# Down projection with weights stationary, two token groups at a time, and seven block products for eight in half of the feature blocks

## The chip, the cores and the metric

The kernel runs on one core of a Trainium2 chip. The metric is the device time of one execution, in microseconds (us); the median of three runs stands for a kernel. The engines are TensorE (PE, with its weight loads PEld), VectorE (DVE), ScalarE (ACT), GpSimd (POOL) and SyncE (SP), which issues nearly all DMA transfers here.

## The reference

A linear attention with decay in blocks of 64 positions gives the tokens, and an MLP with a leaky ReLU follows:

```python
batch, n_heads, seq, head_dim = (4, 8, 768, 64)
for b in range(nb):                       # blocks of 64 positions
    ...
    out[:, :, sl] = intra + inter
    kv_state = lam_block[None, :, None, None] * kv_state + np.einsum('bhsd,bhse->bhde', kb_dec, vb)
# bridge: (B,H,S,D) -> (B*S, H*D)
n_tokens, d_model, d_ff = (3072, 512, 2048)
h = x @ w_in
g = np.maximum(0.01 * h, h)
return (g @ w_out).astype(np.float32)
```

All values are float32. The change concerns the last product, `g @ w_out`: 3,072 tokens by 2,048 features by 512 columns.

## The kernel before

**Three parts for each operand.** The products run on TensorE in a 4-byte float type with fewer significant bits (fp32r). Each operand is therefore written as three such tiles, called h, l and m: h is the operand scaled (by `NEAR`, just below 1) and rounded, l is what h lost, and m is a combination of h and l. Each product of two operands is three matmuls, h by h, l by l and m by m, and the scales are chosen so that a weighted sum of the three is the product to float32 accuracy. `parts` makes them for the weights (ACT or DVE for h, L591 or L593; DVE for l, L596, and m, L602), and `down_load` for the features (ACT L682, DVE L683 and L685).

**Stages.** The attention rounds (chunks of 128 positions) fill the tokens x group by group: six groups of 512 tokens (`NG`, `T`). The features are cut into eight blocks p of 256 (`NP`). `up(g, p)` (L640) multiplies one group by one block of `w_in`, with the weights stationary and 512 tokens streaming; ACT rescales between the m products and the others (L658) and applies the leaky ReLU (L661), and the result `gs` goes to memory as `G[g][p]`, 512 KB with features on the partitions, two halves of 128. Rounds and up blocks are interleaved. Meanwhile `w_out` arrives as words of eight bytes, becomes float32 (`to_float32`, ACT and DVE, from the buffer `raw0`), goes to memory as `WO[p]`, and is read back and split by `w_out_parts` in the last token group of the up stage, after which the weight tiles `W[p]` hold parts of `w_out` instead of `w_in`.

**The down stage** starts when the up stage ends. For each group g and each pair of feature blocks, `down_load` fetches `G[g][p]` into a buffer `graw`, lying where the attention had its tiles, and splits it into one of four ring slots (`NR`), which lie in the two buffers X that the up stage read tokens from (slots 0 and 1 in X[0], 2 and 3 in X[1]). `down` (L700) then multiplies: the stationary operand is a slot's 128 features by 128 tokens, and 512 columns of `W[p]` stream. Each block of 128 tokens has two of the eight PSUM banks, one for h and l and one for m; a bank is complete after all eight feature blocks. Then ACT rescales the first bank into a buffer in SBUF (L722), DVE adds the second to it (L729), and SP stores 256 KB, 128 tokens by 512 columns (L732). The very last block is done in two halves of 256 columns.

**Order.** The class `Plan` takes every instruction with an assumed duration, the names that it reads and writes, and a rank (its place in the list `seq`), and plans by these assumed times which instruction each engine takes next; the instructions are then emitted in the planned order. Each engine works in that order, so an instruction that has to wait holds up all that is behind it on its engine. SP's queue is of this kind too. Loads of the down stage have the rank of eight steps earlier (`plan.rank = n - 8.0`). `move` adds a DMA with a slack that delays its planned place.

Of the kernel before, what the change touches and what calls it, by code (L numbers as in the profile page):

```python
# [8 lines left out]
F32 = mybir.dt.float32  # L9
# [16 lines left out]
S = 4096.0  # L26
# [136 lines left out]
def kernel(  # L163
# [34 lines left out]

    DV = 10
# [21 lines left out]
    bank = {"b10": b1[0], "b11": b1[1], "b2": b2}  # L221
# [3 lines left out]
    raw = [sb([P, 2 * d_model], f"raw{i}") for i in range(NRAW)]  # L225
    lows = [sb([P, d_model], f"low{i}", I32) for i in range(2)]
    w32 = sb([P, 2, d_model], "w32")
    w32f = w32.rearrange("p h n -> p (h n)")
    tt = [raw[-1][:, i * T:(i + 1) * T] for i in range(2)]
    gs = [sb([P, 2, T], f"gs{i}") for i in range(2)]  # L230
    WO = [dram.tile([P, 2 * d_model], F32, name=f"wo{p}", tag=f"wo{p}") for p in range(NP)]
    G = [[dram.tile([P, 2 * T], F32, name=f"g{g}_{p}", tag=f"g{g}_{p}") for p in range(NP)] for g in range(NG)]
# [323 lines left out]
    def to_float32(kind, p, h, dst, key, after=()):  # L556
# [20 lines left out]
        move(1.6, get, after, [f"raw{j}"])  # L577
# [9 lines left out]
    def parts(p, src, keys):  # L587
        wh, wl, wm = W[p]
        def head(e):
            if e == "ACT":  # L590
                nc.scalar.activation(out=wh, in_=src, func=AF.Copy, bias=0.0, scale=NEAR / S)  # L591
            else:
                nc.vector.tensor_scalar(wh, src, NEAR / S, None, op0=ALU.mult)  # L593

        add(("ACT", "DVE"), (1.05, 0.7), head, keys, [f"wh{p}"])
        add("DVE", 1.25, lambda: nc.vector.scalar_tensor_tensor(wl, wh.bitcast(F32), -S, src, op0=ALU.mult, op1=ALU.add),  # L596
            keys + [f"wh{p}"], [f"wl{p}"])
        difference(p)
# [12 lines left out]
    NR = 4  # L611
    graw = [att[:, j * 2 * T:(j + 1) * 2 * T] for j in range(NR)]

# [5 lines left out]
    def w_out_parts(p):  # L619
        j = p % NR  # L620
        add("DMA", 1.5, lambda: nc.sync.dma_start(out=graw[j], in_=WO[p]), [f"WO{p}"], [f"gr{j}"], rank=-3.0)
        parts(p, graw[j], [f"gr{j}"])


    n_t = n_g = 0
    n_b = -EARLY

    def up(g, p, lo=0, hi=GC):
# [20 lines left out]
        for fs in blocks:  # L649
# [11 lines left out]
            add("ACT", ns, lambda b=b, r=r: nc.scalar.activation(out=r, in_=b, func=AF.Prelu, bias=0.0, scale=1.0 / WS, alpha=0.01),  # L661
# [6 lines left out]
    acc = [[z[:, i].rearrange("p y t -> p (y t)") for i in range(2)] for z in (psc, po)] + [  # L668
        [b1[0], b2], [b1[1], pt.rearrange("p y t -> p (y t)")]]
    ACC = [["psc", "psc"], ["po", "po"], ["b10", "b2"], ["b11", "pt"]]  # L670
    ring = [[X[j // 2][z].rearrange("p k t -> p (k t)")[:, j % 2 * 2 * T:(j % 2 + 1) * 2 * T] for z in range(3)] for j in range(NR)]

    def down_load(g, p):
        j = (g * NP + p) % NR
        add("DMA", 1.5, lambda: nc.sync.dma_start(out=graw[j], in_=G[g][p]), [f"G{g}{p}"], [f"gr{j}"])
        h, l, m = ring[j]
        reads = [f"gr{j}"]

        def wr(z):
            return [f"r{z}{j}"] + [f"x{z}{j // 2}{cc}" for cc in range(GC)] if g == 0 and p < NR else [f"r{z}{j}"]  # L680

        add("ACT", 1.05, lambda: nc.scalar.activation(out=h, in_=graw[j], func=AF.Copy, bias=0.0, scale=NEAR), reads, wr("h"))  # L682
        add("DVE", 1.25, lambda: nc.vector.scalar_tensor_tensor(l, graw[j], 1.0, h.bitcast(F32), op0=ALU.mult, op1=ALU.subtract),  # L683
            reads + [f"rh{j}"], wr("l"))
        add("DVE", 1.25, lambda: nc.vector.scalar_tensor_tensor(m, l.bitcast(F32), -S, h.bitcast(F32), op0=ALU.mult, op1=ALU.add),  # L685
            [f"rh{j}", f"rl{j}"], wr("m"))

    def down(g, p):

        nonlocal n_t  # L690
        for tb in range(GC):
            done = p + 2 == NP
            very_last = done and g == NG - 1 and tb == GC - 1

            def go(pps, zs, cols, tb=tb):
                for pp in pps:
                    j = (g * NP + pp) % NR
                    for f in range(2):
                        for z in zs:
                            nc.tensor.matmul(acc[tb][z // 2][:, cols], lhsT=ring[j][z][:, f * T + tb * P:f * T + (tb + 1) * P],  # L700
                                             rhs=W[pp][z][:, f * d_model:(f + 1) * d_model][:, cols],
                                             start=pp == 0 and f == 0 and z != 1, stop=pp == NP - 1 and f == 1,
                                             skip_group_check=True)

            def needs(pps, zs):
                return [f"{x}{z}{y}" for pp in pps for z in zs for x, y in (("r", (g * NP + pp) % NR), ("w", pp))]


            every = slice(0, d_model)
            halves = [slice(0, d_model // 2), slice(d_model // 2, d_model)]  # L710
            one, two = (p,), (p + 1,)
            order = [(one, (0, 1, 2), every), (two, (0, 1, 2), every)]
            if very_last:
                order = [(one + two, (0, 1), every)] + [(one + two, (2,), x) for x in halves]
            for pps, zs, cols in order:
                part_of = f"{halves.index(cols)}" if cols in halves else ""
                add("PE", 0.227 * 2 * len(pps) * len(zs) * (0.53 if part_of else 1.0), lambda pps=pps, zs=zs, cols=cols, go=go: go(pps, zs, cols),
                    needs(pps, ["hlm"[z] for z in zs]) + ([ACC[tb][1]] if part_of else []), sorted({ACC[tb][z // 2] + part_of for z in zs}))
            if done:
                jt, n_t = n_t % 2, n_t + 1  # L720
                t, y = tt[jt], gs[jt][:, 0, :]
                add("ACT", 0.6, lambda t=t, tb=tb: nc.scalar.activation(out=t, in_=acc[tb][0], func=AF.Copy, bias=0.0, scale=(1.0 + 1.0 / S) / U),  # L722
                    [ACC[tb][0]], [f"t{jt}"], rank=-1.5)
                rows = out[(g * GC + tb) * P:(g * GC + tb + 1) * P, :]
                n = 2 if very_last else 1
                for i in range(n):
                    cols = slice(i * d_model // n, (i + 1) * d_model // n)
                    add("DVE", 0.69 / n + 0.08 * (n - 1),
                        lambda t=t, y=y, tb=tb, cols=cols: nc.vector.scalar_tensor_tensor(  # L729
                            y[:, cols], acc[tb][1][:, cols], 1.0 / WS, t[:, cols], op0=ALU.mult, op1=ALU.add),  # L730
                        [f"t{jt}", ACC[tb][1]] + ([ACC[tb][1] + str(i)] if n == 2 else []), [f"gs{jt}{i}" if n == 2 else f"gs{jt}"], rank=-1.5)
                    add("DMA", 0.8 / n, lambda rows=rows, y=y, cols=cols: nc.sync.dma_start(out=rows[:, cols], in_=y[:, cols]),  # L732
                        [f"gs{jt}{i}" if n == 2 else f"gs{jt}"], [], rank=-1.5)

# [83 lines left out]
```

## Time and profile before

| | |
|---|---|
| runs | 610.41, 611.12, 612.04 us; median 611.12 |
| span of the profiled execution | 609.2 us from the first to the last instruction (the median time lies 1.9 us above it) |
| mean granted clock of TensorE | 0.999 |
| busy in the span | PE 98%, PEld 81%, DVE 52%, ACT 44%, POOL 14% |
| the chain that ended last | PE 92%, DVE 4%, DMA 2%, ACT 1% |
| down stage | 343.4 to 605.6 us, PE busy throughout |
| moved | 105.18 MB, mean 173 GB/s |

A share of busy time is an average over stages. In the tables by stretch, each row gives start:end in us, the length, then busy us and number of instructions of PE, PEld, DVE, ACT and POOL, the granted clock, the share of time that the 16 DMA engines were busy, and GB/s. In the groups, a row gives line, engine, operation, out<-in, shape and count, then busy us and the mean ns of one, then the idle time just before them and what ended most of it. A row of the timeline gives the start, the length, the engine and the line, with the idle time before it in brackets. A row of the DMA issues gives the count, the size of each and the median us from issue to landing.

### The profile page before, as it was taken

What the parts mean: (1) busy time and instruction counts of PE and PEld (TensorE: products, weight loads), DVE (VectorE), ACT (ScalarE), POOL (GpSimd) and SP (SyncE); (2) the same over time, 40 slices, a digit from 0 to 9 for tenths busy, and PEclk for the clock granted to TensorE, in tenths of its full rate; (3) what the DMA queues carried; (4) which work ended last, traced back from release to release, by engine and by line L of the source; (5) the groups of instructions that cost most, each with busy time, mean ns of one, the idle gap of its engine ahead of it and who ended that gap; (6) DMA issues with size and microseconds to landing.
All of it is one profiled execution on the core that took longest, in us unless ns stands there. A gap on an engine that the chain in (4) does not pass through costs nothing.

```text
span 609.2 us, 12932 instructions
## 1 busy us (share of the span) xinstructions
PE 597.9 (98%) x5386; PEld 495.6 (81%) x5386; DVE 314.0 (52%) x418; ACT 269.0 (44%) x430; POOL 86.8 (14%) x90
## 2 busy tenths in 40 slices
PE   7899999999999999999999999999999999999997
PEld 6687888888888878888788888888888888888886
DVE  5999764334243426326366745545454544635531
ACT  4688974444455646555577522222222313214111
POOL 1654412104133004104000000000000000000000
PEclk9999999999999999999999999999999999999999
DMA  9998774667888878886686843524333343333201
GB/s 213 232 272 245 221 203 124 173 133 199 199 213 238 212 227 214 216 244 210 233 300 217 290 145 103 173 69 139 138 104 131 112 138 105 138 104 122 86 1 69
DMA packets 147754, 105.18 MB, mean 173 GB/s; under 512 B 123632, under 2 KB 124400, under 8 KB 147696
## 3 DMA queue, kind: packets, MB, share of 16 engines
q1 hardware_dynamic: 147552, 104.36, 58.9%
q8 instruction: 42, 0.69, 0.5%
q14 instruction: 16, 0.13, 0.1%
q10 hardware_dynamic: 144, 0.00, 0.0%
HBM read 68.69 MB, written 35.65 MB: 171 GB/s over the span
## 4 chain that ended last, share of the span: by engine, by line
PE 92%; DVE 4%; DMA 2%; ACT 1%; issue 0%; POOL 0%; SPq 0%; DVEq 0%; ACTq 0%
PE b L640 40%; PE b L700 18%; PE po L700 11%; PE psc L700 11%; PE po L313 4%; PE pt L700 4%; PE psc L313 4%; DMA g<-gs 1%; DMA att<-in_v_dram 1%; DVE w L584 1%; DVE w L585 1%; DVE wm L602 1%; PE pt L403 1%; DMA att<-in_k_dram 1%; DVE wl L596 0%; DVE wh L593 0%
## 5 line engine op out<-in xcount | busy, mean ns | idle before, releaser
L682 ACT ACTIVATE xh<-att 128x1024 fp32r<-128x1024 f32 x48 | 50.7, 1060 | 148.7 <-PE b L700 140.7
L683 DVE SCALAR_TENSOR_TENSOR xl<-att,xh 128x1024 fp32r<-128x1024 f32 x48 | 58.6, 1223 | 98.6 <-ACT xh L682 98.6
L640 PE MATMUL b<-xm,wm 128*128 128x512 f32 (+2 forms) x392 | 104.5, 393 | 0.5 <-ACT b L658 0.5
L640 PE MATMUL b<-xl,wl 128*128 128x512 f32 (+2 forms) x392 | 103.4, 388 | 0.6 <-DVE wl L596 0.6
L640 PE MATMUL b<-xh,wh 128*128 128x512 f32 (+2 forms) x392 | 103.2, 387 | 0.8 <-ACT xh L507 0.8
L640 PEld LDWEIGHTS b<-xh,wh 128*128 128x128 f32 x392 | 73.0, 188 | 15.9 <-ACT xh L507 0.9
L640 PEld LDWEIGHTS b<-xl,wl 128*128 128x128 f32 x392 | 72.8, 188 | 15.6 <-DVE wl L596 1.0
L640 PEld LDWEIGHTS b<-xm,wm 128*128 128x128 f32 x392 | 71.5, 188 | 15.7 <-ACT b L658 0.9
L658 ACT ACTIVATE b<-b 128x512 f32<-128x512 f32 (+2 forms) x97 | 56.1, 580 | 60.3 <-PE b L640 60.1
L661 ACT ACTIVATE gs<-b 128x512 f32<-128x512 f32 (+2 forms) x97 | 56.8, 591 | 44.9 <-PE b L640 38.8
L700 PE MATMUL b<-wl,xl 128*128 128x512 f32 x192 | 74.8, 390 | 0.0
L700 PE MATMUL b<-wh,xh 128*128 128x512 f32 x192 | 74.8, 390 | 0.0
L685 DVE SCALAR_TENSOR_TENSOR xm<-xl,xh 128x1024 fp32r<-128x1024 f32 x48 | 58.7, 1226 | 4.7
L462 POOL TENSOR_TENSOR att<-att 128x256 f32<-128x256 f32 x40 | 35.0, 876 | 57.2 <-DVE att L459 55.9
L700 PEld LDWEIGHTS b<-wl,xl 128*128 128x128 f32 x192 | 36.1, 188 | 7.4
L700 PEld LDWEIGHTS b<-wh,xh 128*128 128x128 f32 x192 | 36.0, 188 | 7.5
L423 POOL TENSOR_TENSOR att<-att 128x512 f32<-128x512 f32 (+1 forms) x20 | 24.2, 1211 | 96.2 <-DVE att L383 47.4
L452 DVE TENSOR_TENSOR att<-psc,att 128x512 f32<-128x512 f32 x24 | 16.5, 690 | 41.0 <-PE psc L313 41.0
L584 DVE TENSOR_SCALAR w<-w 128x512 int32<-128x512 int32 x32 | 19.2, 599 | 35.4 <-ACT w L578 35.3
L700 PE MATMUL po<-wm,xm 128*128 128x512 f32 x96 | 37.4, 390 | 0.0
L700 PE MATMUL po<-wh,xh 128*128 128x512 f32 x96 | 37.4, 390 | 0.0
L700 PE MATMUL po<-wl,xl 128*128 128x512 f32 x96 | 37.4, 390 | 0.0
(73 smaller groups left out, 805.4 us busy)
## 6 DMA issues: line engine op xcount, KB each, us to landing
att<-g SPq DMA_DIRECT2D x48, 512.0 KB, 3.3
g<-gs SPq DMA_DIRECT2D x47, 512.0 KB, 4.0
raw<-in_moe_w_in_dram SPq DMA_DIRECT2D x16, 512.0 KB, 5.4
raw<-in_moe_w_out_dram SPq DMA_DIRECT2D x16, 512.0 KB, 4.7
att<-in_k_dram SPq DMA_DIRECT2D x48, 128.0 KB, 4.2
att<-in_v_dram SPq DMA_DIRECT2D x24, 256.0 KB, 4.4
out_dram<-gs SPq DMA_DIRECT2D x23, 256.0 KB, 2.1
wo<-w SPq DMA_DIRECT2D x8, 512.0 KB, 5.9
```

The lines of the kernel that those rows point to most:

```text
L313: nc.tensor.matmul(dst[HALF[cols]], lhsT=lhsT[HALF[rows]], rhs=rhs[HALF[rows]], start=start, stop=True, skip_group_check=True)
L423: add(eng, us, lambda: e.tensor_tensor(o, x, _bc(pow_q, 2, 2)[:, :, m, :], op=ALU.mult), ["fq", dep], [f"qsT{i}"])
L452: add("DVE", 0.69, lambda: nc.vector.tensor_tensor(sc, psc[:, :, lower, :], decay, op=ALU.mult), ["psc", "fk"], ["sc"])
L462: add("POOL", 0.7, lambda new=new, j=j: nc.gpsimd.tensor_tensor(state[(j + 1) % 4], new, _bc(lam_c, 2, D), op=ALU.mult), [f"st{j % 4}", "f ...
L584: add("DVE", 0.42, lambda: nc.vector.tensor_scalar(d, d, 3, None, op0=ALU.logical_shift_left), [], [key])
L640: nc.tensor.matmul(dst, lhsT=w[z][:, kk * 2 * P + f * P:kk * 2 * P + (f + 1) * P], rhs=x[z][:, kk, toks], start=start and kk == 0, stop=kk ...
L658: add("ACT", ns, lambda b=b: nc.scalar.activation(out=b, in_=b, func=AF.Copy, bias=0.0, scale=S + 1.0), [], [kb], rank=-1.5)
L661: add("ACT", ns, lambda b=b, r=r: nc.scalar.activation(out=r, in_=b, func=AF.Prelu, bias=0.0, scale=1.0 / WS, alpha=0.01), [kb], [f"gs{jg} ...
L682: add("ACT", 1.05, lambda: nc.scalar.activation(out=h, in_=graw[j], func=AF.Copy, bias=0.0, scale=NEAR), reads, wr("h"))
L683: add("DVE", 1.25, lambda: nc.vector.scalar_tensor_tensor(l, graw[j], 1.0, h.bitcast(F32), op0=ALU.mult, op1=ALU.subtract), reads + [f"rh{ ...
L685: add("DVE", 1.25, lambda: nc.vector.scalar_tensor_tensor(m, l.bitcast(F32), -S, h.bitcast(F32), op0=ALU.mult, op1=ALU.add), [f"rh{j}", f" ...
L700: nc.tensor.matmul(acc[tb][z // 2][:, cols], lhsT=ring[j][z][:, f * T + tb * P:f * T + (tb + 1) * P], rhs=W[pp][z][:, f * d_model:(f + 1) ...
```

## The change

The down stage is written anew.

- **Weights stationary, banks transposed.** A bank now holds 128 output columns by the 512 tokens of a group. The stationary operand is a quarter of `W[p]`, and a ring slot streams (`product`). All three matmuls of a product go to one bank, since the m part is made with the factor of its product folded in (`minus`, in place of the one instruction of `difference`: a subtraction on DVE or POOL and a scaling on ACT); the leaky ReLU's scale takes up the rest. So a group of tokens needs four banks, and a pair of groups all eight, called X, Z, Y, V, two of each kind.
- **Seven for eight.** Two groups by two halves of the columns by two halves of the features make a 2x2 block product. For p < 4 (`NS`) it is done with seven block products (`strassen`, units t = 1 to 7 with u = 0, 1 for the two pairs of p; 12 matmuls of 512 columns each) in place of eight. Their operands are sums and differences: of the weights, made in `w_out_parts` (four subtractions of 256 columns per p, L661, and three extra parts in the freed attention and `low` buffers), and of G, made in `sums_of`: two loads of 512 KB, four subtractions of 512 columns on DVE or POOL, two stores of 512 KB to `TS`. There are twelve sets of these, one for each pair of groups and p < 4: the four of pair 0 late in the up stage, those of pairs 1 and 2 during the down stage. Between the units banks are copied (`copy_banks`, ACT) or added (`add_banks`, ACT and then DVE). For p >= 4 `plain` does the ordinary 24 matmuls for each group.
- **Loads.** `unit` loads straight into the m tile of a ring slot (two transfers of 256 KB for a unit of `strassen`, one of 512 KB for `plain`) and splits there: one ACT and two DVE instructions as before. The ring has four slots in pair 0, and a fifth after it, in the freed `raw` buffers. In pair 0 the first units use the slots 0, 1, 0, 1, 2, 3.
- **Leaving.** `leave` transposes a bank by blocks of 32 x 32 on DVE into one of the two halves of `gs0` and stores it by four DMAs of 32 partitions, in pieces of 32 columns (128 bytes). There are 24 banks to store; the very last is done in two halves.
- The first step of `w_out`'s conversion comes one place earlier, and its loads have the slack 0.75 in place of 4.0.

The core of the diff:

```diff
-    tt = [raw[-1][:, i * T:(i + 1) * T] for i in range(2)]
+    TS = [[dram.tile([P, 4 * T], F32, ...) for p in range(NS)] for r in range(NG // 2)]
...
+    def minus(us, x, key):
+        add(("DVE", "POOL"), (us, 1.9 * us), lambda e: ENG[e].tensor_tensor(x(2), x(1).bitcast(F32), x(0).bitcast(F32), op=ALU.subtract), ...)
+        add("ACT", 0.85 * us, lambda: nc.scalar.activation(out=x(2), in_=x(2).bitcast(F32), func=AF.Copy, bias=0.0, scale=1.0 / (S + 1.0)), ...)
...
-    acc = [[z[:, i].rearrange("p y t -> p (y t)") for i in range(2)] for z in (psc, po)] + [...]
+    acc = {"X": flat[:2], "Z": flat[2:], "Y": [b1[0], b2], "V": [b1[1], bank["pt"]]}
+    KINDS = {1: (0, "X"), 5: (1, "V"), 6: (-1, "Z"), 2: (2, "X"), 7: (-2, "Z"), 3: (-3, "Y"), 4: (3, "Z")}
+    BANKS = [[("X", 0), ("X", 1), ("Z", 0), ("Z", 1)], [("Y", 0), ("Y", 1), ("V", 0), ("V", 1)]]
+    slots = [0, 1] + [0, 1, 2, 3] * 4
...
+    def unit(pieces):
+        def go():
+            a = 0
+            for _, src, lo, n in pieces:
+                nc.sync.dma_start(out=ring[j][2][:, a:a + n].bitcast(F32), in_=src[:, lo:lo + n])
+                a += n
...
+        add("DMA", 1.5, go, [x[0] for x in pieces], wr("m"))
+        add("ACT", 1.05, head, [f"rm{j}"], wr("h"))
+        add("DVE", 1.25, low, [f"rm{j}", f"rh{j}"], wr("l"))
+        add("DVE", 1.25, middle, [f"rh{j}", f"rl{j}"], [f"rm{j}"])
...
+    def sums_of(pr, p):
+        for z, kz, g in ((a, ka, 2 * pr), (b, kb, 2 * pr + 1)):
+            move(1.5, lambda z=z, g=g: nc.sync.dma_start(out=z, in_=G[g][p]), [f"G{g}{p}"], kz, slack=WSLACK)
+        for o, u, v, w in ((a[0], b[0], a[0], ka), (b[0], b[1], b[0], kb), (b[1], b[1], a[0], kb), (a[1], a[1], b[1], ka)):
+            add(SUM[0], SUM[1], lambda e="POOL", o=o, u=u, v=v: ENG[e].tensor_tensor(o, u, v, op=ALU.subtract), [], ka + kb)
+        for z, kz, i in ((x[0], ka, 0), (y[0], kb, 1)):
+            move(1.5, lambda z=z, i=i: nc.sync.dma_start(out=TS[pr][p][:, i * 2 * T:(i + 1) * 2 * T], in_=z), kz, ...)
+    def product(dst, j, col, lhs, first=False, n=T):
+        for z in range(3):
+            nc.tensor.matmul(dst, lhsT=lhs(z), rhs=ring[j][z][:, col:col + n], start=first and z == 0, stop=z == 2, ...)
...
+    def leave(g, c, b, kb, k, lo, n):
+        o, n_o = n_o % 2, n_o + 1
+        y = gs[0][:, o, lo:lo + n]
+        add("DVE", 0.1 + 0.6 * n / T, lambda: nc.vector.transpose(out=y, in_=b[:, lo:lo + n]), [kb, k], ...)
+        def store():
+            for a in range(4):
+                nc.sync.dma_start(out=out[g * T + lo:g * T + lo + n, c * P + a * C4:c * P + (a + 1) * C4].rearrange("(b i) j -> i b j", i=C4),
+                                  in_=y[a * C4:(a + 1) * C4, :].rearrange("i (b j) -> i b j", j=C4))
+    def add_banks(d, s):
+        for i in range(2):
+            add("ACT", 0.6, lambda i=i, y=y: nc.scalar.copy(y, acc[s][i]), [ACC[s][i]], key, rank=-1.5)
+            add("DVE", 0.72, lambda i=i, y=y: nc.vector.tensor_tensor(acc[d][i], acc[d][i], y, op=ALU.add), [f"o{i}"], [ACC[d][i]], rank=-1.5)
...
+        if pr:
+            seq += [late[0], s(1, 0), late[1], s(1, 1), ("copy", "Z", "X"), late[2], s(6, 0), late[3], s(6, 1), ("copy", "Y", "Z"),
+                    s(5, 0), s(5, 1), ("add", "Y", "V"), s(7, 0), s(7, 1), ("add", "V", "Z"),
+                    s(3, 0), *soon[0], n(4, 0), s(2, 0), n(5, 0), *soon[1], s(3, 1), s(2, 1), n(6, 0), *soon[2], s(4, 0), s(4, 1), *soon[3], n(7, 0)]
+        else:
+            i = seq.index(("up", NG - 1, NP - 1))
+            seq[i:i] = [s(1, 0)]
+            seq += [s(1, 1), ("copy", "Z", "X"), s(2, 0), s(2, 1), s(3, 0), s(3, 1), s(6, 0), s(6, 1), ("add", "Y", "Z"),
+                    s(5, 0), s(5, 1), ("add", "Y", "V"), ("wp", 4), s(7, 0), s(7, 1), ("add", "V", "Z"), ("wp", 5),
+                    *soon[0], n(4, 0), s(4, 0), *soon[1], ("wp", 6), n(5, 0), s(4, 1), *soon[2], ("wp", 7), n(6, 0), *soon[3], n(7, 0)]
+    seq += [n(p, 1) for p in range(NS, NP)]
```

Lines of the changed kernel that are named below: loads of a ring slot L741, its splits on ACT L746 and on DVE L750 (l) and L754 (m); subtractions of `minus` L610 and its scaling L612; `sums_of` L772 (loads), L775 (subtractions) and L777 (stores); bank copies L857 and additions L862 (ACT) and L863 (DVE); the transposes of `leave` L846 and its stores L850.

Counted in the built order, the down stage had 1,148 matmuls of 512 columns and 8 of 256 (L700); it now has 1,074 and 12 (L781) and two that open banks (L807). The splits of ring steps go from 48 to 66, the loads of ring steps from 48 to 108 DMAs, the stores of the output from 25 to 100, and 24 loads and 24 stores of `sums_of` are new.

## Prediction before the run

> **What bounds the kernel now.** I read the page's head first, then the stretch of the down stage by engine, then its groups and its end. The page's busy row and clock row:
>
> ```profile
> span 609.2 us, 12932 instructions
> PE 597.9 (98%) x5386; PEld 495.6 (81%) x5386; DVE 314.0 (52%) x418; ACT 269.0 (44%) x430; POOL 86.8 (14%) x90
> PEclk9999999999999999999999999999999999999999
> ```
>
> TensorE works 98% of the span at full clock, so only fewer matmuls can save time, and any wait added costs its full length. The table by stretch (the last column pair is DMA share and GB/s; the third row is the down stage):
>
> ```profile
> 130.00:132.00 2.00, 2.00 (x10) 1.68 (x9) 0.96 (x3) 0.73 (x2) 0.00 (x0) 1.00 0.45 71
> 440.00:470.00 30.00, 30.00 (x134) 24.87 (x133) 15.04 (x13) 7.36 (x8) 0.00 (x0) 1.00 0.33 106
> 343.40:605.60 262.20, 262.20 (x1161) 217.26 (x1159) 128.58 (x118) 63.50 (x72) 0.00 (x0) 1.00 0.34 116
> ```
>
> The down stage has no PE wait at all: 262.2 us for 1,148 matmuls of 512 columns and 8 of 256. DVE is half used, POOL idle, DMA at a third. 48 matmuls take 10.88 us in the chain of waits, **0.2267 us each**. The groups that the change multiplies, and the waits of the loads' first step:
>
> ```profile
> L682 ACT ACTIVATE xh<-att 128x1024 fp32r<-128x1024 f32 x48 | 50.7, 1060 | 148.7 <-PE b L700 140.7
> L683 DVE SCALAR_TENSOR_TENSOR xl<-att,xh 128x1024 fp32r<-128x1024 f32 x48 | 58.6, 1223 | 98.6 <-ACT xh L682 98.6
> L685 DVE SCALAR_TENSOR_TENSOR xm<-xl,xh 128x1024 fp32r<-128x1024 f32 x48 | 58.7, 1226 | 4.7
> L452 DVE TENSOR_TENSOR att<-psc,att 128x512 f32<-128x512 f32 x24 | 16.5, 690 | 41.0 <-PE psc L313 41.0
> L383 DVE STREAM_TRANSPOSE att<-att 128x512 f32<-128x512 f32 x11 | 7.2, 678 | 1.1 <-DMA att<-in_q_dram 1.1
> ```
>
> ACT waited 140.7 us for PE to free a ring slot: loads and splits are far ahead. One ring step of 512 KB costs ACT 1.06 and DVE 2.45 us.
>
> **What is removed.** In the built order the 1,148 full matmuls become 1,076 (two of them only open banks), the 8 half ones 12. A half one is 0.139 us (8 in 1.11 us, below). 72 x 0.2267 = 16.3, less 4 x 0.139 = 0.6: **-15.8 us**, 262.2 to 246.4. L722 and L729 (25 outputs) also go, both hidden.
>
> **What is added, and where it is hidden.** Ring steps go from 48 to 66: 18 x 2.45 = 44.1 us of DVE. With 20 of the 48 sum subtractions (0.69 by L452), 14 bank additions (0.69) and the weight sums, DVE in the down stage rises from 128.6 to about 207 of 246 us, an estimate from these rows. That average is below one, but the order is uneven. I counted the built order in steps of 96 matmuls (21.8 us of PE), at row prices. DVE gets 20.0 and 20.3 us in the two steps before the entry, then 27.1, 24.4, 15.7, 9.4, 25.7, 18.5, 13.1, 11.9, 23.6, 16.1, 8.9. Before, it was 10 to 12 per step. DMA at 1.56 us per 512 KB (440-470 moves 3.18 MB in 0.33 x 30 x 16 engine-us, 20 GB/s per engine) needs 32.0 in the first of these and 31.8 in the fifth. So PE waits at the entry, at the two pair boundaries and at the end. The rest (ACT: 10 bank copies, 14 more for the additions, 12 scales; the later L775 on DVE and POOL) lies in steps with slack. In the up stage I cost the first four sets of sums and the weight sums at 0: DVE has 1.5 us or more left per step. If that cover fails, one up step with 24.8 us of DMA would cost up to 3.
>
> **Entry.** Pair 0 runs its first twelve units in a row, 12 matmuls (2.72 us) each, half as long as before per ring step. X[1] belongs to the last up block, so units 2 to 4 share two slots. `s(2,1)` can be loaded only when `s(1,1)` has ended: 3.3 (landing of att<-g, below) + 1.06 + 2.45 + 0.4 of hops = 7.2, less 0.9 of up matmuls and 2.72 of `s(2,0)`: 3.6 us. The two copies Z<-X (0.6 each by L722) fall within it. From there to `s(7,0)`, eight units cost DVE 19.6, with a weight split 1.23, three sums 2.07 and an addition 0.69: 23.6 against 21.8: 1.8. The next unit and three additions take 4.5 against 2.7: 1.8 more. That is 7.2. In this stretch POOL is used for the first time beside DVE's down work: two L610 and five L775, about 11.4 us by the POOL rows (512 columns 1.29). What that costs DVE is seen early in the trace, the same DVE line with and without POOL:
>
> ```profile
> 28.20 1.29 POOL L423 TENSOR_TENSOR att<-att 128x512 f32<-128x512 f32 x1 [1.28 <-ACT att L415]
> 29.44 1.61 POOL L462 TENSOR_TENSOR att<-att 128x256 f32<-128x256 f32 x1
> 28.25 2.31 DVE L602 SCALAR_TENSOR_TENSOR wm<-wl,wh 128x1024 fp32r<-128x1024 f32 x1
> 39.25 1.22 DVE L602 SCALAR_TENSOR_TENSOR wm<-wl,wh 128x1024 fp32r<-128x1024 f32 x1
> ```
>
> DVE lost 1.09 us in 2.31 us of POOL work, 0.47 per us: 11.4 x 0.47 = 5.3. **Entry +12.5.** Bounds: 5.4 (one of the 1.8 hidden, no loss) and 18.6 (DVE loses all 11.4). The 10.2 us by which DMA exceeds this step lie beside this, in the same time.
>
> The Trainium skill (SBUF — State Buffer, "Who interferes with whom") says that a DVE instruction with two SBUF inputs and a GpSimd instruction that reads SBUF exclude each other completely. By that rule the loss would be 11.4 and the total 6.1 us more. The row above shows the loss, but only half of it, so the sum keeps 0.47.
>
> **Pair boundaries.** The new chain: V0 and V1 are transposed (0.68), each is stored by four DMAs of 32 partitions, which must land before the two halves of `gs0` take Y0 and Y1; only then may ACT copy Y<-Z and `s(5,..)`, `s(7,..)` go on. On SP's queue the loads of `s(7,1)` and `s(3,0)` stand behind Y0's stores, which wait for that transpose. Nothing of this kind is in the trace; the nearest rows are the 128-byte pieces of L374:
>
> ```profile
> att<-g SPq DMA_DIRECT2D x48, 512.0 KB, 3.3
> out_dram<-gs SPq DMA_DIRECT2D x23, 256.0 KB, 2.1
> raw<-in_k_dram SPq DMA_DIRECT2D x64, 48.0 KB, 2.7
> 119.29 6.20 SPq L374 DMA_DIRECT2D raw<-in_k_dram  x9
> ```
>
> An L374 issue takes about 0.5 us (0.69 in this run of nine, 0.34 for a whole L732), so one bank occupies SP for 2.0 and lands some 2.1 to 2.7 later. From V0 ready to Y1 copied: 0.7 + 2 x 2.0 + 2.7 + 0.7 + 0.6 = 8.7, against 5.4 of PE work in `s(5,..)` behind the copies of the first bank: about 3. At the first boundary DMA also has the sums of pair 2, 31.8 against 21.8 us, of which the slack of the steps before takes most: I take 4 (2 to 12); at the second 2.7 (2 to 5). **+6.7.**
>
> **Tail.** Now the last matmul ends at 605.61 and the span 3.6 later:
>
> ```profile
> 604.50 1.11 PE L700 MATMUL pt<-wm,xm 128*128 128x256 f32 x8
> 605.71 0.76 DVE L729 SCALAR_TENSOR_TENSOR gs<-pt,raw 128x256 f32<-128x256 f32 x2 [1.72 <-PE pt L700]
> ```
>
> After: V0, V1, Y0, Y1 are finished 1.36 us apart and share two output halves. From V0's end: transposed 0.8, issued 2.8, landed 4.9; V1 issued 4.8, landed 6.9; Y0 transposed 5.7, issued 7.7; Y1's halves issued 9.7 and 11.7, landed 13.8. PE ends at 4.2, so the tail is 9.6: **+6.0**; with issues of 0.34 and landing 1.7 it is +2.7, with 0.69 and 2.7 +10.2.
>
> **Sum.** 12.5 + 6.7 + 6.0 = 25.2 against 15.8: +9.4. The span becomes 618.6; the median of 611.12 lies 1.9 outside the profiled span of 609.2, so 620.5 us. All low ends give 12.1 (607.4), all high ends 45.8 (641). It turns at 15.8.
>
> **Rivals.** *Faster: the waits are covered.* DVE and DMA run so far ahead after the first wait of 3.6 that neither POOL nor the boundaries reach PE; only it and the tail's 6.0 remain: 9.6 - 15.8 = -6.2, 604.9 us. For it: the average of 84% on DVE, and 140.7 us of slack in ACT's waits. Against: that slack was in a ring whose slots lasted 5.4 us, the entry leaves two slots, and two steps ask more than 21.8 of DVE. 0.22.
>
> *Slower than forecast: the small stores are dear.* At 130-132, 142 KB of such reads kept the engines busy 14.4 us, 13 ns a piece; a bank is 2,048 pieces, 1.7 us of 16 engines, 13.3 a pair. If a write of 128 bytes takes twice that, each boundary gets 13 us more, about half of it in front of awaited loads: +7, about 627.5. Nothing in the trace writes such pieces, neither for nor against. 0.12. The Trainium skill (DMA: Bandwidth & Descriptors, "Specifications") says that transfers under 512 bytes are read, modified and written; no run here shows it yet.
>
> *No change*: waits of 14 to 17.6: 0.08. That the change does not do what it says is excluded by the count in the built order. The forecast itself has 0.58.
>
> **Numbers.** Measurement can tell about 0.3% (1.8 us). Slower is 0.58 + 0.12 = 0.70, same 0.08, faster 0.22. The range reaches down to the rival's 604.9 and up past the dear stores: 605 to 634; the likeliest case alone has 613 to 630.
>
> **What would show it.** In the profile after: matmuls from L781 at the same 0.2267 where they run on; PE idle of 10 us or more in the first 45 us of the down stage, ended by DVE; a longer L750/L754 where POOL works; idle before `s(5,..)` and `s(7,..)`, released by ACT copies or by loads; a tail near 9.6 with SP issuing L850. It would be wrong if the entry is without the 3.6 wait, if L850 issues take much under 0.4, or if PE's granted clock falls below 1.00 behind a long wait, which no row here has.

## The result, and the profile after

The changed kernel takes **651.12 us** (median of four runs, 650.08 to 652.48) against 610.76 on the same chip: ratio 1.0652, interval [1.063, 1.0675]. It was forecast slower, at 620.5; it lies 17 us above the top of the range, 634. The page of the profile after, the same rows as before:

```profile
span 650.6 us, 13371 instructions
...
PE 602.8 (93%) x5318; PEld 488.3 (75%) x5318; DVE 413.8 (64%) x507; ACT 298.4 (46%) x463; POOL 151.4 (23%) x124
...
PEclk9999999999999999999999789989997999999998
```

PE is down to 93%, and its clock is no longer full: slices of 8 and 7 stand where the down stage begins and again in its middle. The table by stretch answers to the row 343.40:605.60 of before, which had no idle time (entry; the stretch after it; first boundary; plain units; second boundary; the last stretch):

```profile
360.20:412.00 51.80, 40.54 (x145) 30.35 (x145) 48.88 (x39) 24.28 (x28) 20.70 (x10) 0.87 0.79 279
412.00:440.00 28.00, 25.23 (x102) 19.89 (x102) 21.56 (x18) 4.19 (x4) 8.30 (x4) 0.94 0.63 228
440.00:520.00 80.00, 70.72 (x294) 56.58 (x293) 58.00 (x47) 22.15 (x25) 24.93 (x13) 0.96 0.79 232
520.00:560.00 40.00, 39.93 (x176) 32.61 (x175) 26.03 (x24) 12.74 (x13) 0.00 (x0) 1.00 0.67 182
560.00:600.00 40.00, 38.14 (x164) 30.36 (x163) 33.75 (x33) 14.81 (x17) 0.00 (x0) 1.00 0.61 167
600.00:641.40 41.40, 41.40 (x189) 34.42 (x187) 18.71 (x19) 6.38 (x6) 0.00 (x0) 1.00 0.39 99
```

At the entry DVE is busy 48.9 of 51.8 us, and the granted clock is 0.87. At 600 to 641, without sums and with enough loads ahead, PE runs through at full clock: the matmuls themselves cost what was forecast.

**Where 41.4 us went.** The last up matmul ends at 360.2 with 26 matmuls of the down stage (5.9 us) among those before it; before, at 345.65 with 6 (1.4): the up stage lost 10.0. From 360.2 there remain 1,050 matmuls and 12 half ones, 239.7 us, which should end at 599.9; they end near 641.3: 41.4 lost. Waits make 28.5 of it: the timeline's 21 idle gaps (those over 0.15 us) sum to 25.2, and each wait costs 0.16 more than its gap, because a matmul is 0.39 long and the next one would have started 0.2267 after it. Sums of idle time in the down stage are counted in this way below, from start to start, unless gaps are named. The lower clock makes 10.3: the trace grants half the clock for 23.9 us (362.8 to 366.2, 369.6 to 376.4, 383.3 to 386.7, 427.6 to 431.1 and 492.5 to 499.3); in 3.2 of them PE waited, and half of the other 20.6 is lost. The remaining 2.6 is matmuls slightly further apart at full clock; I did not assign it. The tail is 9.1 in place of 3.6: 5.5. With the 15.8 saved: 10.0 + 28.5 + 10.3 + 2.6 + 5.5 - 15.8 = 41.1, against 41.4 in the spans.

The up stage first. These are waits of ACT from 150 to 345 us in the changed kernel (total, times, longest); before, ACT never waited for a load of `w_out`:

```profile
ACT w L584 <- DMA raws<-in_moe_w_out_dram: 7.4, 4, 3.2
ACT lows L586 <- DMA raws<-in_moe_w_out_dram: 4.6, 3, 3.0
```

L704 and L707 stand behind these on ACT, and PE waits for them. All of PE's waits from 150 to 345 us come to 8.4, and half a clock from 178.5 to 181.9, behind a wait of 1.96, takes 1.7 more:

```profile
PE b L686 <- ACT b L704: 3.8, 5, 2.0
...
PE b L686 <- ACT gs L707: 1.9, 2, 1.7
```

Then the clock. The timeline of PE at the entry; the bracket is the idle time before the matmul:

```profile
362.20 0.50 PE L781 MATMUL psc<-xh,wh 128*128 128x512 f32 x1 [1.84 <-ACT po L857]
...
364.01 0.63 PE L781 MATMUL psc<-xm,wm 128*128 128x512 f32 x1
364.44 0.63 PE L781 MATMUL psc<-xh,wh 128*128 128x512 f32 x1
364.87 0.63 PE L781 MATMUL psc<-xl,wl 128*128 128x512 f32 x1
```

The starts are 0.43 apart in place of 0.2267, for about 3 us after the wait. After the wait of 1.72 at 397.47 they were not. What decides is worked out under `holds` below.

Third, DVE and POOL at the entry, the same 1,024-element instruction that took 1.22 alone, and the subtraction L775 that takes 1.30 on POOL alone:

```profile
374.89 2.19 DVE L754 SCALAR_TENSOR_TENSOR xm<-xl,xh 128x1024 fp32r<-128x1024 f32 x1
377.01 4.53 DVE L750 SCALAR_TENSOR_TENSOR xl<-xm,xh 128x1024 fp32r<-128x1024 f32 x2
```

```profile
373.86 2.15 POOL L775 TENSOR_TENSOR gs<-gs 128x512 f32<-128x512 f32 x1
376.08 2.15 POOL L775 TENSOR_TENSOR gs<-gs,w 128x512 f32<-128x512 f32 x1
378.31 2.15 POOL L775 TENSOR_TENSOR w<-w,gs 128x512 f32<-128x512 f32 x1
```

The two take turns: one of each in 2.2 us, so the split is 0.97 longer than alone and the subtraction 0.85.

Last, SP: the stores of the sums wait for POOL, ahead of ring loads in the same queue (waits of SP's queue, 345 to 645 us):

```profile
SPq L741 <- PE po L781: 42.5, 25, 5.3
SPq L777 <- POOL w L775: 30.7, 6, 9.8
SPq L850 <- DVE gs L846: 29.6, 10, 8.6
```

### The profile page after: what moved, and what is told of

It is laid out like the page before. It is cut to its first block, busy times and chain, and to the rows that moved or that the text cites. A ratio compares the mean times of both kernels' runs of the same rounds, so it can differ in the third digit from the quotient of the medians.

```text
span 650.6 us, 13371 instructions
## 1 busy us (share of the span) xinstructions
PE 602.8 (93%) x5318; PEld 488.3 (75%) x5318; DVE 413.8 (64%) x507; ACT 298.4 (46%) x463; POOL 151.4 (23%) x124
## 4 chain that ended last, share of the span: by engine, by line
PE 65%; DMA 15%; DVE 7%; SPq 3%; issue 3%; POOL 3%; ACT 2%; DVEq 0%; POOLq 0%; ACTq 0%
PE b L686 30%; PE psc L781 8%; PE po L781 8%; PE b L781 8%; PE po L319 3%; PE psc L319 3%; DMA raws<-g 3%; DMA xm<-ts 2%; PE pt L781 2%; DMA raws<-in_moe_w_out_dram 2%; DMA w<-g 2%; DVE xl L750 2%; SPq L850 2%; DMA ts<-w 2%; DMA att<-in_k_dram 1%
## 5 line engine op out<-in xcount | busy, mean ns | idle before, releaser
L746 ACT ACTIVATE xh<-xm 128x1024 fp32r<-128x1024 f32 x56 | 59.3, 1060 | 113.2 <-DMA xm<-g 54.7
L750 DVE SCALAR_TENSOR_TENSOR xl<-xm,xh 128x1024 fp32r<-128x1024 f32 x56 | 79.7, 1425 | 33.0 <-ACT xh L746 33.0
L754 DVE SCALAR_TENSOR_TENSOR xm<-xl,xh 128x1024 fp32r<-128x1024 f32 x56 | 81.0, 1448 | 2.8
L704 ACT ACTIVATE b<-b 128x512 f32<-128x512 f32 (+2 forms) x97 | 56.0, 582 | 49.6 <-PE b L686 49.5
L707 ACT ACTIVATE gs<-b 128x512 f32<-128x512 f32 (+2 forms) x97 | 56.9, 590 | 38.9 <-PE b L686 34.9
L429 POOL TENSOR_TENSOR att<-att 128x512 f32<-128x512 f32 (+1 forms) x20 | 24.2, 1212 | 108.5 <-DVE att L389 58.0
L425 POOL TENSOR_TENSOR att<-att 128x512 f32<-128x512 f32 (+1 forms) x23 | 27.5, 1198 | 44.1 <-DMA att<-in_k_dram 25.7
L781 PE MATMUL psc<-xh,wh 128*128 128x512 f32 x80 | 33.4, 418 | 4.5 <-ACT xh L746 2.6
L781 PE MATMUL psc<-xl,wl 128*128 128x512 f32 x80 | 32.9, 411 | 3.5 <-DVE xl L750 3.5
L781 PE MATMUL psc<-xm,wm 128*128 128x512 f32 x80 | 33.2, 415 | 2.0 <-DVE xm L754 2.0
L319 PEld LDWEIGHTS po<-att 64*64 64x64 f32 x1472 | 27.6, 137 | 9.8 <-issue 7.1
L319 PE MATMUL po<-att 64*64 64x64 f32 x1472 | 33.3, 224 | 1.3 <-DVE att L497 0.6
L775 POOL TENSOR_TENSOR w<-gs,w 128x512 f32<-128x512 f32 x7 | 14.2, 2036 | 79.4 <-DMA gs<-g 79.4
```

Of the source, the lines that this page charges most:

```text
L319: nc.tensor.matmul(dst[HALF[cols]], lhsT=lhsT[HALF[rows]], rhs=rhs[HALF[rows]], start=start, stop=True, skip_group_check=True)
L425: lambda e="POOL": ENG[e].tensor_tensor(kr[nr], kr[nr], _bc(pow_k, 3, D)[nr], op=ALU.mult), ["fk"], [f"k{i}"])
L429: add(eng, us, lambda: e.tensor_tensor(o, x, _bc(pow_q, 2, 2)[:, :, m, :], op=ALU.mult), ["fq", dep], [f"qsT{i}"])
L704: add("ACT", ns, lambda b=b: nc.scalar.activation(out=b, in_=b, func=AF.Copy, bias=0.0, scale=S + 1.0), [], [kb], rank=-1.5)
L746: nc.scalar.activation(out=h, in_=m.bitcast(F32), func=AF.Copy, bias=0.0, scale=NEAR)
L750: nc.vector.scalar_tensor_tensor(l, m.bitcast(F32), 1.0, h.bitcast(F32), op0=ALU.mult, op1=ALU.subtract)
```

## The experiments

Each changes the changed kernel by the lines shown, unless another is named. Ratios are to the kernel before on the same chip; in us, the medians are compared with 651.1.

**The up stage (up_restored).**

```diff
-        move(1.6, get, after, [f"raw{j}"], slack=WSLACK)
+        move(1.6, get, after, [f"raw{j}"], slack=SLACK)
-    ... ("r", 11), ("wo", 0, 0, ["G14"]), ("up", 1, 6) ...   nxt, n_out, begin = 3 * GC, 1, len(seq)
+    ... ("r", 11), ("up", 1, 6) ...                           nxt, n_out, begin = 3 * GC, 0, len(seq)
```

> The changed kernel with the loads of w_out as before: slack 4.0 and the first step at its old place. Theory (slack): the up stage lost 10.0 us because the conversion's ACT instructions (L584, L586) are queued before their load has landed and hold the rescaling L704 and L707 that PE waits for; with the old slack PE has under 1 us of waits between 150 and 345 us, and the time falls by 8 to 10, to about 642. Rival (merged buffers, or the sums of pair 0 made late in the up stage): the up stage still loses 8 or more, and the time stays at 651.

674.58 us, ratio 1.1034 [1.1017, 1.105]: 23 us slower, a miss. The cause of the up stage's waits was right: from 150 to 345 us PE's idle gaps are now 0.9 us in all. The sums of pair 0 were not the cause, as their first subtraction stands at 310.5 us in the changed kernel, behind its long waits (168 to 228 us). But without the early loads this subtraction starts at 341.6, and the entry pays more (PE's waits, total, times, longest):

```profile
PE po L781 <- ACT xh L746: 24.2, 3, 12.5
```

In the chain of waits the units stand behind `DMA ts<-raws`, `SPq L772` and `DMA xm<-ts`. So the 10 us in the up stage went with sums that were ready earlier; neither place is free.

**The sums of pairs 1 and 2 (no_sums, sums_no_arith, sums_no_dma).**

```diff
# no_sums
-            sums_of(*x[1:])
+            if x[1] == 0:
+                sums_of(*x[1:])
-            j = unit([(f"TS{pr}{p}{i // 2}", TS[pr][p], i * T, T) for p in ps_])
+            j = unit([(f"TS0{p}{i // 2}", TS[0][p], i * T, T) for p in ps_])
# sums_no_arith: the loop over the four subtractions
+        ...[:4 if pr == 0 else 0]:
# sums_no_dma: the loops over the two loads and the two stores, and units read TS[0]
+        ...[:2 if pr == 0 else 0]:
```

> The changed kernel without the sums of G for pairs 1 and 2: their units read the sums of pair 0, so 32 subtractions, 16 loads and 16 stores of 512 KB are left out, all of the down stage. Theory (sums): of the 41 us that PE lost in the down stage, the first 19 at the entry and the 14 at the first boundary hang on POOL's subtractions, on the stores that wait for them on SP's queue ahead of the ring loads, and on the 16 MB moved; the down stage loses under 15 and the time is about 625. Rival (my entry and boundary without POOL: two slots, splits on DVE, banks that must leave): the down stage still loses 14 to 20 by itself and clock lost after long waits stays, time 632 to 640.

623.32 us, ratio 1.0189 [1.0161, 1.0218]: 27.8 less, as the first theory had it. The first boundary lost almost nothing, the second half a microsecond, and the entry kept 9.3 us of idle time from 360 to 400, with a clock loss of 2.6. (My entry without POOL was 7.2.)

> The changed kernel with the 32 subtractions of the sums for pairs 1 and 2 left out; their loads and stores stay, so the 16 MB move as before. Without the sums altogether the time was 623.3, with them 651.1: 27.8 us to share out. Theory (arithmetic: POOL and DVE take turns, and SP's queue waits for POOL before it may issue the stores, ring loads behind them): most of the 27.8 goes, time 625 to 633. Rival (traffic: DMA is full at the entry and ring loads land late): the time stays at 640 to 648.

634.02 us, ratio 1.0368 [1.0351, 1.0385]: 17.1 less than with the subtractions, so bytes and queue alone cost 10.7 over no_sums. Between the two expectations, nearer to the first.

> The counterpart: the 32 subtractions stay, on whatever the two buffers hold, and the loads and stores of the sums of pairs 1 and 2 are left out (their units read those of pair 0). POOL and DVE have the same work, SP waits for none of it. Theory (queue: it is the stores waiting on SP's queue, not the lock by itself): 624 to 630. Rival (lock: POOL's 32 instructions cost DVE some 20 us, of which the entry pays most): 635 to 645. Rival (traffic): 624 to 628, and then the run without subtractions stays above 640.

648.29 us, ratio 1.0626 [1.0579, 1.0673]: arithmetic alone costs 25.0 over no_sums. The lock is the expectation that came nearest, 3 us below the measured time. Without loads to wait for, POOL runs its subtractions in one row from 361 to 436 us, where DVE has its entry, and PE's idle time there ends with DVE's L750 and L754 (24.4 of 27.8 us of gaps). Bytes 10.7 and arithmetic 25.0 do not add up to 27.8. The subtractions also stand elsewhere than in the changed kernel, where they are spread from 372 to 513 us, so 25.0 is their price crowded into the entry, and not a share of the 27.8.

**Where the arithmetic is done (dve_sums), and who issues its stores (stores_on_pool).**

```diff
# dve_sums: sums_of, minus and w_out_parts
-    SUM = (("DVE", "POOL"), (0.67, 1.25))
+    SUM = (("DVE",), (0.67,))
# stores_on_pool
-            move(1.5, lambda z=z, i=i: nc.sync.dma_start(out=TS[pr][p]..., in_=z), ...)
+            move(1.5, lambda z=z, i=i: (nc.gpsimd if pr else nc.sync).dma_start(out=TS[pr][p]..., in_=z), ...)
```

> The changed kernel with every subtraction of sums_of, minus and w_out_parts on DVE, so POOL does nothing in the down stage. Theory (lock: DVE and POOL exclude each other, so work on POOL costs DVE nearly its whole length): DVE gets 28 more subtractions at 0.69 (19 us) and loses the 24 us by which L750 and L754 were longer than 1.22; L750 falls to 1.23 and the stores of the sums wait less on SP; time the same or up to 10 us less, 641 to 651. Rival (POOL relieves DVE): the down stage loses 15 us more, time 660 to 670. Rival (DMA is the limit at the entry): no change within 4 us.

646.3 us, ratio 1.0576 [1.0561, 1.0592]: 4.8 less, as the lock has it. L750 fell from 1.43 to 1.22 us. POOL had relieved DVE of nothing: from 360 to 640 us DVE is busy for 206.2 us with all the subtractions, and was busy for 207.1 with POOL's help.

> The changed kernel with the 16 stores of the sums of pairs 1 and 2 issued on POOL's own queue in place of SP's, all else as it is. Theory (queue): no ring load stands behind a store that waits for a subtraction any more; 8 to 15 us less, 636 to 643. Rival (traffic, lock): within 4 us of 651, as bytes and arithmetic are the same.

646.12 us, ratio 1.0562 [1.0525, 1.0599]: 5 less, the four runs spread from 642.5 to 648.4. SP's queue costs something, less than I expected of it; from 450 to 510 us PE still lost 11.6 us of idle time and 7.2 of clock.

**Weights stationary alone (plain_only).** The up part is as in up_restored; NS = 0, the sequence is

```diff
+    for g in range(NG):
+        for p in range(NP):
+            seq.append(("n", g // 2, p, g % 2) if p < NP - 1 else ("l", ...))
```

> Weights stationary alone: all eight feature blocks by the ordinary products (NS = 0), no sums, no extra weight parts, no copies between banks; the loads of w_out as before. 1,140 full and 24 half-size matmul slots are as many as before. Theory: a group's banks are free for a whole group before they are used again, so PE waits under 2 us in the down stage and only the tail of 9.2 in place of 3.6 is left: 611 + 5.6 = 617. Rival (stores of 128-byte pieces, or transposes on DVE, disturb the ring loads at every group): 622 or more, with waits at five boundaries.

618.33 us, ratio 1.0115 [1.0098, 1.0132], as expected. PE was busy 261.24 of 262 us from 345 to 607, with one wait of 0.8:

```profile
345.00:607.00 262.00, 261.24 (x1157) 216.05 (x1156) 129.23 (x116) 53.92 (x54) 0.00 (x0) 1.00 0.42 116
```

So the new orientation, the transposes, `minus` and the stores in pieces of 128 bytes cost the tail (9.5 us in place of 3.6) and little else: 5.9 of the 7.1 us between the medians, and one wait.

**The clock by itself (holds).** plain_only with ACT copying one bank onto itself in the middle of each group:

```diff
+        elif x[0] == "hold":
+            d, i = BANKS[x[1]][3]
+            for _ in range(x[2]):      # 5, 6, 7, 8, 10, 13
+                add("ACT", 0.6, lambda d=d, i=i: nc.scalar.copy(acc[d][i], acc[d][i]), [], [ACC[d][i]], rank=-1.5)
```

> The clock by itself. The kernel of plain_only (618.3), in which PE never waits for long, with ACT copying one bank onto itself 5, 6, 7, 8, 10 and 13 times in the middle of the six groups, so that PE has to wait there: idle of about 1.1, 1.7, 2.3, 2.9, 4.1 and 5.8 us, 18 in all. Reading of the changed kernel: matmuls after a wait of 1.84 us or more took 0.43 in place of 0.2267 for some 3 us, after 1.72 or less they did not; so the first two holds cost their idle time alone, each of the four longer ones 1.8 to 2.8 more: 643 to 648 us. Rival (the slow matmuls came from something else that was full at the time, DMA or the SBUF side): all at 0.2267, 636 us. By the Trainium skill (TensorE: Matmul & The Clock Gate) only gaps over about 3 us lower the clock: then only the last two holds, 640 us.

645.46 us, ratio 1.0556 [1.0527, 1.0586]: 27.1 more than plain_only (two runs only, 646.51 and 644.41). The six waits in PE's timeline:

```profile
370.41 0.50 PE L781 MATMUL po<-xh,wh 128*128 128x512 f32 x1 [1.71 <-ACT po L935]
416.53 0.50 PE L781 MATMUL pt<-xh,wh 128*128 128x512 f32 x1 [1.63 <-ACT pt L935]
462.58 0.50 PE L781 MATMUL po<-xh,wh 128*128 128x512 f32 x1 [2.91 <-ACT po L935]
511.51 0.79 PE L781 MATMUL pt<-raws,wh 128*128 128x512 f32 x1 [2.83 <-ACT pt L935]
561.57 0.79 PE L781 MATMUL po<-xh,wh 128*128 128x512 f32 x1 [5.57 <-ACT po L935]
613.83 0.79 PE L781 MATMUL pt<-xh,wh 128*128 128x512 f32 x1 [5.84 <-ACT pt L935]
```

The first two were followed by matmuls at 0.2267; the other four cost 1.7, 1.5, 2.1 and 1.3 us more. A wait alone, with all other work as in plain_only, lowers the clock: the rival is out. The Trainium skill (TensorE: Matmul & The Clock Gate, "Why this matters for your kernels") advises against gaps of over about 3 us; here 2.83 in this run and 1.84 in the changed kernel lowered it, and the measurement decides.

But the length of a wait does not decide alone, and 1.84 is no threshold. The same wait for the copy in no_sums, and one of 3.10 in `lag` (below), were followed by matmuls 0.23 apart:

```profile
361.75 0.50 PE L781 MATMUL psc<-xh,wh 128*128 128x512 f32 x1 [1.84 <-ACT po L857]
```

```profile
589.85 0.47 PE L783 MATMUL b<-xh,att 128*128 128x512 f32 x1 [3.10 <-DVE b L865]
```

And in the changed kernel the clock was halved at 383.3 behind waits of 1.64 and 0.76 with a single matmul between them. In the clock records of all the traces here the clock changes only at the edges of stretches of 3.41 us, which run on evenly through a trace. Take the stretches at full clock from 60 us on and PE's idle time in each. Where PE was idle for over 1.9 us of a stretch, the next one was at half clock, 42 times of 42; where it was idle for 0.7 to 1.5 us, never, in 56; between these, 10 times of 22. A wait that lies across an edge is divided between two stretches: that of 3.10 gave 1.4 us to one and 1.7 to the next. A stretch at half clock costs at most 1.7 us. Behind the waits of 2.91 and 2.83 there was one, behind those of 5.57 and 5.84 two, the first of them mostly within the wait.

**Less crowding (two_pairs, one_pair).** Pair 0 (in one_pair also pair 1) by ordinary products; up part as before the change; sums on DVE. The extra weight parts, and the changed second block of `W[p]`, are made in the down stage; the last group leaves through four output halves and the queues of SP and ACT.

```diff
# one_pair; two_pairs has the pairs 1 and 2 in this form, with s(2,u) where the changed kernel has it
+        if pr == 2:
+            seq += [late[0], s(1, 0), late[1], s(1, 1), ("copy", "Z", "X"), late[2], s(6, 0), late[3], s(6, 1), s(2, 0), s(2, 1), ("copy", "Y", "Z"), ...]
+        elif pr == 1:
+            seq += [*late, n(0, 0), n(1, 0), ("ts", 2, 0), n(2, 0), ..., ("ts", 2, 3), ("wx", 2), n(3, 1), ("wx", 3)]
```

> A version made from the readings so far. Pair 0 is done by ordinary products, pairs 1 and 2 with seven for eight; the loads of w_out are as before the change; the extra weight parts and all sums are made in the down stage, on DVE, the sums of a pair spread over the pair before it; the last group leaves through four output buffers and two queues. 48 products fewer: -10.9. If only long runs of units without prepared loads and crowded sums cost, the up stage and the first entry lose 0 to 2, two boundaries 2 to 3 each, the tail is 4 to 6 in place of 3.6: 603 to 608 us. Rival (a unit of 2.72 us on a ring of four or five slots is too short for load, split and landing, wherever it stands): each of the two pairs loses 8 or more and the time is 615 to 625.

628.35 us, ratio 1.0271 [1.0234, 1.0308]: above both, nearer to the rival. The up stage lost nothing (PE waited 0.3 from 150 to 345 us), but from 330 us on PE lost 15.0 us of idle time and 6.9 of slow clock, at the entry and at both boundaries.

> Seven for eight only in the last pair: its sums, the extra weight parts and the changed parts are made during the 174 us of the first two pairs, on DVE; s(2,0) and s(2,1) stand ahead of the copy Y<-Z, to give 5.4 us more cover while the last banks of pair 1 leave; ring, up stage and last group as in two_pairs. 24 products fewer than before: -5.4; the tail is 5.7 in place of 3.6. If crowding of DVE, DMA and SP's queue was what cost, the boundary and the rest lose 0 to 2: 608 to 610 us, at or a little below before. Rival (units of 2.72 us with 2.45 us of DVE each wait wherever they stand): 612 to 618.

623.99 us, ratio 1.0207 [1.0185, 1.0229]: neither. After a first wait of 0.8, PE waited twice:

```profile
514.38 0.79 PE L792 MATMUL po<-xh,att 128*128 128x512 f32 x1 [5.18 <-ACT po L873]
...
559.95 0.77 PE L792 MATMUL b<-xh,att 128*128 128x512 f32 x1 [5.48 <-DVE b L879]
```

In the chain both lead to a ring load: the copy stood on ACT behind the split of a load that landed 5.6 us after its issue, the addition on DVE behind splits of loads of 5.5 us. So I tried the order.

**The order (lag, one_pair_lag, two_pairs_lag, one_pair_all_lag).** In `unit`, the planner takes a ring load to land later:

```diff
+        plan.slack = 2.5
         add("DMA", 1.5, go, [x[0] for x in pieces], wr("m"))
+        plan.slack = 0.0
```

> The changed kernel with one number more: the planner takes 2.5 us longer for a ring load to land (they took 4.6 to 5.8 us in the changed kernel, it reckons with 2.0 to 3.5), so that copies and additions of banks, transposes and sums stand ahead of the splits of late loads on ACT and DVE. Work, bytes and buffers are the same. Theory (order: on queues that keep their order a bank operation that PE needs stands behind a split whose load is late): 8 to 20 us less, 631 to 643. Rival (work: DVE, POOL's lock and DMA are full at the entry and the boundary, in whatever order): within 5 us of 651.

661.06 us, ratio 1.0834 [1.0792, 1.0876]: 10 us slower, a miss of both. This change of order does not help the changed kernel; from 345 us on PE's idle time is 35.0 us in place of 28.6, and the clock takes 12.9 in place of 10.3. Why later splits are waited for longer I did not trace further.

> one_pair with the same 2.5 us. There PE waited only twice, 5.2 us for a copy Z<-X that stood behind the split of a load landing 5.6 us after its issue on ACT, and 5.5 us for an addition behind three splits on DVE, with 4.7 us of slow clock after them. Theory (order): both go, 608 to 612 us. Rival (the ring itself is too slow there): 618 or more.

617.55 us, ratio 1.0099 [1.0074, 1.0124]: 6.4 less, between the two. Both long waits are gone; 2.5 us stay at the boundary, and a new wait of 4.4 with 1.8 of slow clock came at the entry, behind a subtraction for the extra weight parts whose load took 5.9 us.

> two_pairs with the same 2.5 us. Theory (order): its 15 us of waits and 8 of slow clock fall by half or more, 610 to 618. Rival (work): DVE is at about nine tenths in its first two pairs, so the waits stay, 623 to 630.

629.52 us, ratio 1.0297 [1.0273, 1.0322]: no change against two_pairs, as the rival has it. That it is the work is not shown by this alone: another order might do better.

> one_pair_lag, whose first wait (4.4 us and 1.8 of slow clock) stood behind a subtraction for the extra weight parts on DVE, waiting 5.9 us for its load: now the loads of these parts and of the sums are planned 4.0 us later as well, the subtraction of minus may go to POOL as in plain_only, and the last group leaves by three queues. Theory (order): the first wait falls to the 0.9 of plain_only, 2 to 3 us stay at the boundary, the tail is 4 to 5: 609 to 612 us, no slower than before. Rival (work): 615 to 618 as in one_pair_lag.

622.35 us, ratio 1.0192 [1.0174, 1.021]: a miss of both, and worse than one_pair_lag. The entry is back at 0.9, but the boundary lost 7.5 us of idle time, the clock took 6.6, and the tail was 5.8 with three queues (5.3 with two in one_pair_lag). Several things were changed at once here, so which of them did it is not shown. Moving the planned order moves the waits; no version came below the kernel before.

## Why the prediction was wrong

**Right.** The direction, the 15.8 saved, the tail (9.6 forecast, 9.1 measured), the second boundary (2.7 forecast, 2.5 idle at a granted clock of 1.00), and the idle time of the entry: 12.5 forecast, 12.5 measured from 360 to 412. That this last number agrees is luck. The first wait was not the one I computed: the copy Z<-X and the late load of `s(2,u)` gave 1.84 + 1.39 + 2.73 in place of 3.6. Without the sums the entry still lost 9.3 where I had 7.2, and POOL worked there for 20.7 us where I had 11.4. Two slips of the prediction do not move its sum much: 512 KB at 20 GB/s an engine take 1.64 us, not 1.56, and a half-size matmul follows the last after 0.12 us, not 0.139.

**The clock, put at nothing: 10.3 in the down stage,** and 1.7 of the 10.0 in the up stage. The prediction took a granted clock below 1.00 after a wait as something that would prove it wrong, since no row of before has it. No row of before could have it: there PE never waits. That was a missing price for waits, not evidence of none. The holds put it at 1.3 to 2.1 for each wait of 2.8 us or more; in the changed kernel 1.84 was enough at one place, and the two stretches behind the wait of 3.83 at 493.47 cost 2.9.

**The up stage, put at 0 (up to 3): 10.0.** I checked the cover by counting busy time and DMA time per step, and the diff's line with the slack 0.75 in place of 4.0 was not priced. The slack is not a cost but a place in ACT's queue: the conversion was put ahead of its load, and ACT holds L704 and L707 behind it. Taking back the slack and the earlier first step together (up_restored) removed these waits and cost more at the entry, where the sums came later.

**The first boundary, put at 4 (2 to 12): 10.2 idle and 2.9 of clock,** and 3.3 idle with 1.7 of clock between it and the entry (412 to 440), where I had none. I let the slack of the steps before take the sums of pair 2. But the sums are not spread: each set follows the last as soon as its two buffers are free, and its stores stand on SP's queue ahead of ring loads until POOL is done. With no sums both places lost almost nothing.

**POOL, right in kind and too cheap.** I took 0.47 us of DVE for each us of POOL, and 1.29 for a subtraction. The measured loss is 0.40 per us (21.8 us over 98 splits from 345 to 600, 53.9 of POOL), but the subtraction takes 2.15, so that one costs DVE 0.86 on average and 0.97 where the two take turns (2.19 less 1.22), not the 0.6 of 0.47 x 1.29. The Trainium skill's rule (SBUF — State Buffer, "Who interferes with whom") agrees with that in kind: each holds the other up. DVE loses 0.97 of the 1.30 that the subtraction takes alone. POOL did 20.7 us at the entry, not 11.4. What it cost there cannot be told from the rest.

**The rivals.** "The waits are covered" was far off: the average of 84% on DVE said nothing, as the entry stood at 94%. "The small stores are dear" is out: plain_only has all of them and one wait of 0.8, and from 625 to 637 us in the changed kernel, with only these stores in flight, 56 GB/s at a share of 0.32 is 672 KB in 61 engine-us, 11.7 ns for each piece of 128 bytes. The range failed since the clock and the up stage, 20.3 us together, bring the forecast of 620.5 to 640.8, past its top of 634; the first boundary and the stretch before it bring most of the rest. The top was also below the 641 that the prediction's own high ends add up to.

**What stays open.** How the 28.5 of idle time divide between DVE's work, the lock, bytes and SP's queue: without the bytes 25.0 us over no_sums stay, without the arithmetic 10.7. What the clock does between 1.5 and 1.9 us of idle time in a stretch is open too. And whether an order exists in which one pair pays: 24 products give 5.4 us, and the tail and the boundary took them in every version here.

## What to carry to other kernels

Price a change by the engine with the least room in the tightest stretch: a unit of 2.72 us of PE with 2.45 of DVE leaves 0.27, and at the entry, with DVE busy for 94% of the time, sums, additions and weight splits had no room. Where PE never waited before, the profile cannot show what a wait costs; here a wait of 1.84 us or more could halve the clock behind it, and several short waits close together did so too. A planner's assumed times are part of the kernel: a load assumed earlier than it lands puts its consumer at the head of a queue that keeps its order, and everything behind it waits.

## What the runs showed of the hardware

- The granted clock changes at the edges of even stretches of 3.41 us. After one in which PE was idle for over 1.9 us the next was at half clock (42 of 42), with matmuls 0.43 apart in place of 0.2267; after 0.7 to 1.5 us of idle time it stayed full (56 of 56, from 60 us on in each trace). So a wait of 1.84 us lowered it in one kernel and not in another, and one of 3.10 did not. In `holds`, waits of 2.8 to 5.8 us lost 1.3 to 2.1 more.
- A DVE instruction with two inputs in SBUF beside a subtraction on POOL: 2.2 us in place of 1.22, and 2.15 in place of 1.30 on POOL; without POOL (dve_sums) 1.22 again.
- Stores in pieces of 128 bytes: 11.7 ns a piece over 16 engines, with a median of 1.9 us from issue to landing for one DMA of 64 KB.
